# Linear attention and SiLU projections on one core: one turned q in another bank, state scalings and one sum of g placed later, three products and one subtraction in another order

## The chip, the cores and the metric

The kernel runs on one core of one Trainium2 chip. A core has five engines with a queue each: TensorE (PE; its weight loads are shown as PEld), VectorE (DVE), ScalarE (ACT), GpSimd (POOL) and SyncE (SP, which only issues transfers here). The metric is the device time of one execution in microseconds (us).

## The reference, cut to what matters

Four sequences of 768 tokens with 8 heads of 48 go through a gated linear recurrence; its output, 3072 tokens by 384, goes through two matrix products with SiLU between them.

```python
for t in range(S):        # q, k, v, alpha: (4, 8, 768, 48)
    state = alpha[:, :, t, :, None] * state + einsum('bhd,bhe->bhde', k[:, :, t], v[:, :, t])
    y[:, :, t] = einsum('bhd,bhde->bhe', q[:, :, t], state)
x = y.transpose(0, 2, 1, 3).reshape(3072, 384)
h = x @ w_in              # (384, 2048)
g = h / (1 + exp(-h))
out = g @ w_out           # (2048, 384)
```

The two weights are in 64 bits in memory and are converted on the chip.

## The kernel before, in words

**Chunks and steps.** The tokens are cut into 24 chunks of 128 tokens (6 per sequence). A loop over steps runs four stages on different chunks: at step n the scores of chunk n-1, the products of chunk n, the values and states of chunk n-1. `products` (and `quotient`) makes running products of alpha by two scans (L760, L790), the scaled k (`kp`, L771, later L775 and L777) and the scaled q (`p`, L797). `scores` multiplies `p` and `kp` on TensorE, copies the result to g-shaped tiles (L844, later L850 and L853), masks it on GpSimd (L845, L857), and scales the sequence's state for this chunk (L864, four ScalarE instructions). `values` multiplies with v and the state and copies the result to `xt` (L903); `states` makes the state's addition from `kn` and v (TensorE, then L920).

**Turning.** The scans need alpha, k and q with tokens in the free dimension. For chunks 0 to 7 `bring` turns them on TensorE into PSUM (L398). For chunks 8 to 23 they are loaded in pieces and VectorE turns them (L724); one buffer (`turn`) holds k, then q, then the flipped `kp` (L807) that goes through memory to become `kn`. Turning k or q also issues the load of the next chunk's.

**PSUM.** Eight banks: three rotate for the attention (`ps_a`), three serve the w_in products (`ps_m`), two the w_out products (`ps_o`). For chunks 0 to 3 `bring` takes k and q to the `ps_o` banks (chunk 1: `ps_m`), from chunk 4 on to `ps_a`.

**The two projections.** Groups of 4 chunks, in two halves of 256 tokens. Groups 0 and 1 are computed plainly (`enter_plain`: w_in products, silu L963). Groups 2 to 5 use 20 block products instead of 24 (`enter`, twice a group, each for one pair of quarter columns): sums of blocks of x (`sums_x`, SUMS_X, L596 to L601) and of w_in (SUMS_W) are multiplied in the order of PRODUCTS; each `add` takes the next pair and accumulates into bank a, b or c; `copy` takes a bank to SBUF on ScalarE (L990, to s[i] or the single buffer `part`), `tt` combines on VectorE (L998), and `silu` follows (L995). `side_by_side` adds two column halves of g (L1073). `leave` makes the w_out products of a half in seven steps with seven products of half size in place of eight, with differences (L1087), partial results u (L1113, L1118, L1128, L1130, L1139), and stores (L1094, L1096, L1099).

**Order.** `enter` and `leave` are generators that are cut by `yield` into pieces; `both` puts one step of `leave` ahead of each step of `enter`, and `fill` advances them between the stages by a due count. TensorE runs in the order in which it is written. Other engines' instructions are ordered by a scheduler, except where `settled` (first part), `in_order` or `tc.keep_in_program_order` fixes the written order. Between the stages `audit` loads alpha and the weights once more and reduces them on VectorE (L713), to check their range; a branch at the end goes to a general version if it fails.

```python
def bring(n, names="akq"):            # L726; n < NA = 8 is turned on TensorE
            if n < GB and name != "a":     # L738, GB = 4
                at = "kq".index(name)
                ps[name] = (bank(at) if n == 1 else out_bank(at, 512)).rearrange("p (j c) -> p j c", c=C)
            else:
                ps[name] = ps_attn()
```

Of the kernel before, what the change touches and what calls it, by code (L numbers as in the profile page):

```python
# [13 lines left out]
ALU = mybir.AluOpType  # L14
# [5 lines left out]
def general(  # L20
# [326 lines left out]
)  # L347

PRODUCTS = (
    (11, 9), (3, 6), (14, 6), (18, 15), (5, 11), (17, 8), (9, 14), (7, 10), (10, 3), (19, 12),  # L350
    (2, 16), (0, 10), (12, 9), (15, 0), (6, 16), (13, 13), (16, 4), (8, 1), (1, 7), (4, 5),
)

# [2 lines left out]
def quotients(  # L356
# [20 lines left out]
    dve, act, gps = nc.vector, nc.scalar, nc.gpsimd  # L377

    late = {}
# [7 lines left out]
    def settled(ins):  # L387

        return tc.keep_in_program_order(ins) if stated[0] else ins
# [21 lines left out]
    GB = 4  # L411
# [26 lines left out]
    def out_bank(i, n):  # L438
        return outs[i].tile([128, 512], F32, name="ps_o")[:, 0:n]

    def ps_attn(n=C):
        return ps_a.tile([128, 512], F32, name="ps_a").rearrange("p (j c) -> p j c", c=n)
# [4 lines left out]
    def idle(n):  # L447

        for _ in range(n):
            pe.matmul(spin[:, 0:C], lhsT=ident, rhs=ident, start=True, stop=True)  # L450
# [267 lines left out]
    def tokens(t):  # L718

        return t[:, 1 : NP * W + 1].rearrange("p (j c) -> p j c", c=W)[:, :, 0:C]  # L720

    def turned(x, to):
        x = x[:, 32:].rearrange("p (g j d) -> p g j d", j=4, d=D)
        dve.transpose(to.rearrange("p g (b j) -> p g j b", j=4), x[:, :, :, 0:32])  # L724

    def bring(n, names="akq"):  # L726

        c = ctxs[n]
        sg = seg[0 if late else n % 2]
        ps = c.setdefault("ps", {})  # L730

        for name in names:
            if n >= NA:
                if name == "a":
                    turned(c[name], tokens(sg))
                    load(n + 1, "a")
                continue
            if n < GB and name != "a":  # L738

                at = "kq".index(name)  # L740
                ps[name] = (bank(at) if n == 1 else out_bank(at, 512)).rearrange("p (j c) -> p j c", c=C)
            else:
                ps[name] = ps_attn()
            if n == 0 and name != "a" or n == 1 and name != "q":
                idle(2)
            for j in range(NP):
                pe.transpose(ps[name][:, j, :], c[name][:, 2 * j : 2 * j + 2, :], ident)
            if name == "a":
                settled(act.copy(tokens(sg), ps[name]))  # L749
# [69 lines left out]
    def scores(n):  # L819
        c = ctxs[n]  # L820
        ci, b = c["ci"], c["b"]
        ps = [ps_attn() for _ in range(2)]

        for j in (0, 2, 1, 3):
            for e in range(2 if n >= NA else 1):
                for u in range(2):
                    r = slice(64 * u, 64 * u + D)
                    at = slice(CH * e, CH * e + CH) if n >= NA else slice(0, C)  # L830
                    t = slice(CH * (e ^ j // 2) if n >= NA else 0, C)
                    pe.matmul(ps[u][at, j, t], lhsT=c["kp"][r, j, at], rhs=c["qp"][r, j, t],
                              start=True, stop=True)
        if n == 1:

            room = gpool.tile([128, 4, 2, TB], F32, name="g").rearrange("p a b n -> p (a b n)")
            c["room"] = room[:, 2 * NP * C :]
        g = (room[:, 0 : 2 * NP * C] if n == 1 else decayed).rearrange(
            "p (u j c) -> p u j c", u=2, j=NP)
        swapped = decayed.rearrange("p (o u j c) -> p o u j c", o=2, u=2, j=NP // 2)  # L840
        c["g"] = (lambda u, j: g[:, u, j, :]) if n < NA else (
            lambda u, j: swapped[:, j // 2, u, j % 2, :])
        for u in range(2 if n < NA else 0):
            settled(act.copy(g[:, u], ps[u]))  # L844
            gps.affine_select(g[:, u], g[:, u], pattern=[[0, NP], [1, C]], compare_op=ALU.is_ge,  # L845
                              fill=0.0, base=0, channel_multiplier=-1)
        if n >= NA:
            ps = [x.rearrange("p (o j) c -> p o j c", o=2) for x in ps]
            for u in range(2):
                act.copy(swapped[:, :, u, :, CH:], ps[u][:, :, :, CH:])  # L850
            for r, o in earlier:
                for u in range(2):
                    act.copy(swapped[r, o, u, :, 0:CH], ps[u][r, o, :, 0:CH])  # L853
            for at, half in ((CH, later), (0, earlier)):
                for r, o in half:
                    x = swapped[r, o].rearrange("p u j c -> p (u j) c")[:, :, at : at + CH]
                    gps.affine_select(x, x, pattern=[[0, NP], [1, CH]],  # L857
                                      compare_op=ALU.is_ge, fill=0.0, base=0, channel_multiplier=-1)
        if n != 1:
            back(n)  # L860
        if ci > 0:
            s = st[b].rearrange("p j u e -> p j (u e)")
            for j in range(NP):
                mul = act.mul(s[:, j], s[:, j], least[:, n, j : j + 1])  # L864
                if late:
                    tc.keep_in_program_order(mul)


# [79 lines left out]
    def bank(i, n=512):  # L948
        return banks[turn[i]].tile([128, 512], F32, name="ps_m")[:, 0:n]
# [21 lines left out]
    def enter(grp, pair):  # L971
        g_tiles(grp, pair)
        halves = [gts[grp, h, pair] for h in range(2)]

        s = [halves[o % 2][:, o // 2] for o in range(8)]
        todo = iter(PRODUCTS)

        def new(i):
            return bank(i).rearrange("p (e n) -> p e n", e=2)

        def add(ps, first=False):
            w, x = next(todo)
            for e in range(2):
                pe.matmul(ps[:, e], lhsT=block_w(w)[:, 2 * pair + e], rhs=block_x(grp, x),
                          start=(first and e == 0), stop=(e == 1), skip_group_check=True)

        def copy(ps, to=None):
            if to is None:
                to = late["part"].tile([128, 2, TB], F32, name="part")
            act.copy(to, ps)  # L990
            return to

        def silu(h, i):
            x = halves[h][:, i : i + 2]
            act.activation(x, x, AF.Silu)  # L995

        def tt(to, a, b, op=ALU.add):
            dve.tensor_tensor(to, a, b, op)  # L998

        a, b, c = [new(i) for i in range(3)]  # L1000
        add(a, True)
        copy(a, s[6])
        add(b, True)
        copy(b, s[2])
        add(c, True)
        tt(s[6], s[6], copy(c), ALU.subtract)
        yield
        add(a)
        t = copy(a)
        add(b)  # L1010
        copy(b, s[4])
        add(c)
        copy(c, s[7])
        tt(s[7], s[7], t, ALU.subtract)
        yield
        add(a)
        copy(a, s[5])
        add(b)
        copy(b, s[3])
        tt(s[5], s[5], s[3])  # L1020
        add(c)
        copy(c, s[0])
        yield
        add(a)
        tt(s[4], a, s[4])
        b = new(1)
        add(b, True)
        add(b)
        copy(b, s[1])
        yield  # L1030
        c = new(2)
        add(c, True)
        tt(s[2], s[2], copy(c), ALU.subtract)
        a = new(0)
        add(a, True)
        tt(s[6], a, s[6])
        silu(0, 2)
        add(b)
        tt(s[5], copy(b), s[5], ALU.subtract)
        yield  # L1040
        add(c)
        tt(s[1], c, s[1])
        tt(s[3], s[1], s[3], ALU.subtract)
        a = new(0)
        add(a, True)
        tt(s[2], a, s[2])
        add(b)
        tt(s[7], b, s[7])
        silu(1, 2)
        yield  # L1050
        add(c)
        combine(s[1], -1, s[1], -1, s[0])
        tt(s[0], c, s[0])
        silu(0, 0)
        a = new(0)
        add(a, True)
        tt(s[3], a, s[3])
        silu(1, 0)
        turn.append(turn.pop(0))
        for h in range(2):  # L1060
            side_by_side(grp, h, pair)
        yield

    def cells(grp, h, pair, m, k):

        return gts[grp, h, pair][:, k::2, :, m * C : (m + 1) * C]
# [3 lines left out]
    def side_by_side(grp, h, pair):  # L1070

        x = cells(grp, h, pair, 1, 0)
        settled(dve.tensor_tensor(x, x, cells(grp, h, pair, 1, 1), ALU.add))  # L1073

    def leave(grp, h):

# [227 lines left out]
    for step in range(5, STEPS):  # L1304
# [6 lines left out]
        for slot, group in enumerate(stages):  # L1311
            for stage, lag in group:
                n = step - lag
# [9 lines left out]
            if step * SLOTS + slot == (NA + 1) * SLOTS - 1:  # L1323
                x = decayed.rearrange("p (o i c) -> p o i c", o=2, c=C)
# [87 lines left out]
```

## Time and profile before

| | us |
|---|---|
| median of 3 runs | 553.72 (553.66 to 554.34) |
| the profiled execution | 553.72 |
| its span, from the first to the last instruction | 552.0 |
| TensorE busy, first matmul at 1.6, last ends 547.1 | 539.4 |
| VectorE busy | 446.9 |
| ScalarE busy | 208.2 |
| GpSimd busy | 79.0 |
| TensorE, w_out products (`ps_o`), all | 233.4 |
| TensorE, w_in products (`ps_m`), all but the start | 249.1 |

A line of the timeline reads: start and length in us, engine, line of the kernel, operation, tile written and tiles read, shapes, count, and in brackets how long the engine sat idle before it and what ended that. TensorE rows of one kind are merged; the end of such a row overlaps the next one. A wait is put down to the instruction whose semaphore came last.

### The profile page before, as it was taken

What the parts mean: (1) busy time and instruction counts of PE and PEld (TensorE: products, weight loads), DVE (VectorE), ACT (ScalarE), POOL (GpSimd) and SP (SyncE); (2) the same over time, 40 slices, a digit from 0 to 9 for tenths busy, and PEclk for the clock granted to TensorE, in tenths of its full rate; (3) what the DMA queues carried; (4) which work ended last, traced back from release to release, by engine and by line L of the source; (5) the groups of instructions that cost most, each with busy time, mean ns of one, the idle gap of its engine ahead of it and who ended that gap; (6) DMA issues with size and microseconds to landing.
All of it is one profiled execution on the core that took longest, in us unless ns stands there. A gap on an engine that the chain in (4) does not pass through costs nothing. (4 is left out here: it accounts for less than half of the span.)

```text
span 552.0 us, 12718 instructions
## 1 busy us (share of the span) xinstructions
PE 539.4 (98%) x5068; PEld 491.9 (89%) x5068; DVE 446.9 (81%) x801; ACT 208.2 (38%) x466; POOL 79.0 (14%) x146
## 2 busy tenths in 40 slices
PE   8999999999999999999999999999999999999996
PEld 7787888998899899899999999988998999999996
DVE  5999789974999899997998986998883796955531
ACT  3555654123333344354354253353263342332200
POOL 4111000131211202111011021021131000001000
PEclk9999999999999999999999999999999999999999
DMA  9999762253545434455445654717642136500000
GB/s 214 305 224 216 218 186 54 57 153 90 140 130 140 131 83 119 122 136 152 113 126 145 177 148 110 199 24 181 181 130 90 54 86 173 168 21 15 17 28 27
DMA packets 99218, 70.11 MB, mean 127 GB/s; under 512 B 56272, under 2 KB 88656, under 8 KB 99152
## 3 DMA queue, kind: packets, MB, share of 16 engines
q1 hardware_dynamic: 97232, 65.30, 45.9%
q0 software_dynamic: 1920, 3.93, 2.1%
q8 instruction: 41, 0.67, 0.5%
q14 instruction: 25, 0.20, 0.1%
HBM read 61.34 MB, written 7.86 MB: 125 GB/s over the span
## 5 line engine op out<-in xcount | busy, mean ns | idle before, releaser
L394 PE MATMUL ps_o<-w_out,g 128*128 128x192 f32 x768 | 133.7, 328 | 0.0
L394 PEld LDWEIGHTS ps_o<-w_out,g 128*128 128x128 f32 x768 | 125.8, 190 | 2.5 <-DVE o L1096 0.2
L394 PE MATMUL ps_m<-xt,w_in 128*128 128x256 f32 x480 | 111.9, 381 | 1.0 <-ACT xt L903 0.6
L394 PEld LDWEIGHTS ps_m<-xt,w_in 128*128 128x128 f32 x480 | 89.7, 190 | 13.6 <-ACT xt L903 0.8
L394 PE MATMUL ps_o<-wt,g 128*128 128x192 f32 x576 | 99.7, 326 | 0.0
L394 PEld LDWEIGHTS ps_o<-wt,g 128*128 128x128 f32 x576 | 95.1, 190 | 1.5
L394 PE MATMUL ps_m<-xc,w_in 128*128 128x256 f32 x288 | 70.7, 382 | 0.0
L394 PEld LDWEIGHTS ps_m<-xc,w_in 128*128 128x128 f32 x288 | 53.7, 190 | 7.0 <-DVE g L998 0.3
L995 ACT ACTIVATE g<-g 128x1024 f32<-128x1024 f32 x32 | 33.1, 1056 | 61.0 <-DVE g L998 60.9
L1087 DVE TENSOR_TENSOR g<-g 128x512 f32<-128x512 f32 x72 | 49.9, 707 | 6.8 <-PE ps_o L394 6.8
L857 POOL TENSOR_SCALAR_AFFINE_SELECT g<-g 64x256 f32<-64x256 f32 x64 | 36.3, 567 | 124.1 <-ACT g L850 105.4
L1099 POOL DMA_DIRECT2D out_dram<-o x40 | 22.1, 552 | 214.7 <-DVE o L1096 110.7
L394 PE MATMUL ps_m<-xc,wx 128*128 128x256 f32 x192 | 50.1, 383 | 1.0 <-DVE xc L600 1.0
L990 ACT COPY g<-ps_m 128x512 f32<-128x512 f32 x64 | 36.6, 589 | 37.0 <-PE ps_m L394 36.9
L394 PEld LDWEIGHTS ps_m<-xc,wx 128*128 128x128 f32 x192 | 35.2, 190 | 5.2 <-ACT u L1118 1.2
L998 DVE TENSOR_TENSOR g<-ps_m,g 128x512 f32<-128x512 f32 x56 | 37.0, 681 | 3.2 <-PE ps_m L394 2.7
L760 DVE TENSOR_TENSOR_SCAN u<-al,one 128x516 f32<-128x516 f32 x24 | 30.1, 1254 | 6.9 <-ACT al L749 6.6
L990 ACT COPY part<-ps_m 128x512 f32<-128x512 f32 x32 | 18.9, 590 | 37.3 <-PE ps_m L394 24.0
L963 ACT ACTIVATE g<-ps_m 128x512 f32<-128x512 f32 x32 | 19.0, 595 | 35.5 <-PE ps_m L394 35.1
L790 DVE TENSOR_TENSOR_SCAN p<-al,inv 128x516 f32<-128x516 f32 x24 | 30.0, 1250 | 1.0 <-PE ps_a L394 0.3
L713 DVE TENSOR_REDUCE seen<-bits 128x1 f32<-128x512 int32 (+1 forms) x33 | 26.3, 824 | 5.5 <-DMA bits<-in_moe_w_in_dram 5.5
L1096 DVE TENSOR_TENSOR o<-ps_o,u 128x192 f32<-128x192 f32 x24 | 8.5, 353 | 24.9 <-PE ps_o L394 23.0
(134 smaller groups left out, 653.6 us busy)
## 6 DMA issues: line engine op xcount, KB each, us to landing
bits<-in_moe_w_in_dram SPq DMA_DIRECT2D x24, 512.0 KB, 4.7
bits<-in_moe_w_out_dram SPq DMA_DIRECT2D x16, 384.0 KB, 3.8
at<-in_alpha_dram SPq DMA_DIRECT2D x64, 96.0 KB, 2.6
kt<-in_k_dram SPq DMA_DIRECT2D x64, 96.0 KB, 2.5
qt<-in_q_dram SPq DMA_DIRECT2D x64, 96.0 KB, 2.6
bits<-in_alpha_dram SPq DMA_DIRECT2D x9, 512.0 KB, 4.1
out_dram<-o POOLq DMA_DIRECT2D x40, 96.0 KB, 2.6
flips<-turn SPq DMA_DIRECT2D x12, 256.0 KB, 2.4
```

Of the source, the lines that this page charges most:

```text
L394: in_order(nc.tensor.matmul(*args, **kw))
L713: dve.tensor_reduce(seen[kind][which][:, i : i + 1], x, axis=AX, op=op, apply_absolute_value=True))
L760: settled(dve.tensor_tensor_scan(u[:, end - 1 :: -1], sg[:, end:0:-1], one[:, end:0:-1], 0.0, ALU.mult, ALU.add))
L790: settled(dve.tensor_tensor_scan(p[:, 0:end], sg[:, 0:end], iv[:, 0:end], 0.0, ALU.mult, ALU.add))
L857: gps.affine_select(x, x, pattern=[[0, NP], [1, CH]], compare_op=ALU.is_ge, fill=0.0, base=0, channel_multiplier=-1)
L963: settled(act.activation(gts[grp, h, pair][:, i : i + 2, q % 2, :], ps, AF.Silu))
L990: act.copy(to, ps)
L995: act.activation(x, x, AF.Silu)
L998: dve.tensor_tensor(to, a, b, op)
L1087: dve.tensor_tensor(cells(grp, h, pair, *to), cells(grp, h, pair, *x), cells(grp, h, pair, *y), ALU.subtract)
L1096: dve.tensor_tensor(o, x, y, ALU.add)
L1099: (gps if grp < NG - 1 else nc.sync).dma_start(out[r : r + C, c * HO : (c + 1) * HO], o)
```

## The change

Five edits, none of which adds or removes an instruction with work:

- The turned q of chunk 6 goes to the second `ps_o` bank, as it does for chunks 0, 2 and 3, in place of a `ps_a` bank.
- The four state scalings of chunk 6 keep their written order on ScalarE; the scheduler had put them a step earlier. They now stand behind the copy of `kn` of chunk 6.
- The sum of g (`side_by_side`) of group 1, second half, first pair, keeps its written order; on VectorE it now stands behind k's and q's turning for chunk 9 and their products, ahead of the flip, where it stood ahead of the turning.
- In every call of `enter`, the second round of products runs c, b, a in place of a, b, c: PRODUCTS has (17, 8) and (18, 15) exchanged, and the copies to s[7], s[4] and `part` follow in that order.
- In group 2, first pair, the subtraction into s[3] stands behind the addition into s[2].

On GpSimd and SyncE the order of the instructions is the same as before.

```diff
 PRODUCTS = (
-    (11, 9), (3, 6), (14, 6), (18, 15), (5, 11), (17, 8), (9, 14), (7, 10), (10, 3), (19, 12),
+    (11, 9), (3, 6), (14, 6), (17, 8), (5, 11), (18, 15), (9, 14), (7, 10), (10, 3), (19, 12),
...
-            if n < GB and name != "a":
+            if n < GB and name != "a" or n == 6 and name == "q":
...
                 mul = act.mul(s[:, j], s[:, j], least[:, n, j : j + 1])
-                if late:
+                if late or n == 6:
                     tc.keep_in_program_order(mul)
...
-        add(a)
-        t = copy(a)
+        add(c)
+        copy(c, s[7])
         add(b)
         copy(b, s[4])
-        add(c)
-        copy(c, s[7])
-        tt(s[7], s[7], t, ALU.subtract)
+        add(a)
+        tt(s[7], s[7], copy(a), ALU.subtract)
         yield
...
         tt(s[1], c, s[1])
-        tt(s[3], s[1], s[3], ALU.subtract)
+        late_3 = (grp, pair) == (2, 0)
+        if not late_3:
+            tt(s[3], s[1], s[3], ALU.subtract)
         a = new(0)
         add(a, True)
         tt(s[2], a, s[2])
+        if late_3:
+            tt(s[3], s[1], s[3], ALU.subtract)
...
-        settled(dve.tensor_tensor(x, x, cells(grp, h, pair, 1, 1), ALU.add))
+        total = dve.tensor_tensor(x, x, cells(grp, h, pair, 1, 1), ALU.add)
+        if (grp, h, pair) == (1, 1, 0):
+            tc.keep_in_program_order(total)
+        settled(total)
```

## The prediction

> **What bounds the kernel now.** I read the page first, then the waits of TensorE alone, then the timeline around each wait.
>
> ```profile
> span 552.0 us, 12718 instructions
> ...
> PE 539.4 (98%) x5068; PEld 491.9 (89%) x5068; DVE 446.9 (81%) x801; ACT 208.2 (38%) x466; POOL 79.0 (14%) x146
> ```
>
> TensorE is busy for 539.4 of 552.0 us. What can be won is the rest, and in it only the places where TensorE waits for another engine. Before 80 us these belong to the start and the change doesn't touch them. The waits view of TensorE (who is waited for: us, times, longest) has the later ones:
>
> ```profile
> PE ps_m L394 <- DVE xc L600: 1.0, 1, 1.0
> PE ps_a L394 <- DVE kp L771: 0.8, 2, 0.5
> PE ps_a L394 <- DVE p L797: 0.7, 2, 0.5
> ...
> PE ps_m L394 <- DVE g L998: 0.4, 1, 0.4
> ```
>
> One of the two waits for `p` lies in the start. The timeline shows each of the others with the instruction that ends it.
>
> Place A, steps 6 and 7 of the chunk loop (start, duration, engine, line, tiles, idle before):
>
> ```profile
> 83.95 0.69 DVE L771 TENSOR_TENSOR kp<-ps_a,u 128x512 f32<-128x512 f32 x1
> 83.95 1.17 ACT L864 ACTIVATE st<-st,least 128x96 f32<-128x96 f32 x4 [1.63 <-DVE least L763]
> ...
> 84.69 0.55 PE L394 MATMUL ps_a<-vn,kn 128*32 128x48 f32 x32 [0.54 <-DVE kp L771]
> ...
> 85.03 0.46 ACT L903 COPY xt<-ps_a 128x384 f32<-128x384 f32 x1
> ...
> 85.53 8.04 PE L394 MATMUL ps_m<-xt,w_in 128*128 128x256 f32 x36 [0.29 <-ACT xt L903]
> ...
> 102.96 0.69 DVE L771 TENSOR_TENSOR kp<-ps_a,u 128x512 f32<-128x512 f32 x1
> ...
> 103.71 0.55 PE L394 MATMUL ps_a<-vn,kn 128*32 128x48 f32 x32 [0.28 <-DVE kp L771]
> ```
>
> The state product `vn,kn` of chunk 5 waits at 84.69 for `kp` of chunk 6 (83.95 + 0.69 = 84.64), because its bank held k of chunk 6. The next w_in product waits at 85.53 for the copy of `xt` (ends 85.49), which stands on ScalarE behind four state scalings (1.17 us). At 103.71 the same state product of the next step waits for `kp` of chunk 7 (ends 103.65).
>
> Place B, the second chunk that is turned on VectorE (chunk 9):
>
> ```profile
> 136.32 0.69 DVE L1073 TENSOR_TENSOR g<-g 128x512 f32<-128x512 f32 x1 [7.63 <-ACT g L963]
> ...
> 140.10 0.69 DVE L797 TENSOR_TENSOR p<-turn,p 128x512 f32<-128x512 f32 x1
> ...
> 140.94 0.90 PE L394 MATMUL ps_a<-p,kp 48*64 48x128 f32 x32 [0.48 <-DVE p L797]
> ```
>
> VectorE sits idle for 7.6 us until 136.32 because the sum of g waits for ScalarE's silu; k's and q's turning stand behind it, and the scores (`p,kp`) at 140.94 wait for the last of them.
>
> Place C, group 2:
>
> ```profile
> 225.83 1.28 DVE L998 TENSOR_TENSOR g<-ps_m,g 128x512 f32<-128x512 f32 x2
> ...
> 226.57 1.13 PE L394 MATMUL ps_m<-xt,w_in 128*128 128x256 f32 x4 [0.40 <-DVE g L998]
> ...
> 231.72 0.46 ACT L903 COPY xt<-ps_a 128x384 f32<-128x384 f32 x1
> ...
> 232.44 0.79 PE L394 MATMUL ps_a<-p,kp 48*64 48x128 f32 x26
> ```
>
> The last w_in product waits at 226.57 for the first of the two L998 at 225.83, which reads its bank. Further on, the scores at 232.44 start just after the copy of `xt` that ends at 232.18.
>
> Place D, group 4. The quarter sum of x that TensorE waits for, and then the next place where TensorE and VectorE meet:
>
> ```profile
> 364.94 0.41 DVE L600 TENSOR_TENSOR xc<-xc,xt 128x256 f32<-128x256 f32 x1
> ```
>
> ```profile
> 392.82 0.69 DVE L713 TENSOR_REDUCE seen<-bits 128x1 f32<-128x512 int32 x1 [1.50 <-DMA bits<-in_moe_w_in_dram]
> ...
> 397.41 0.34 DVE L1096 TENSOR_TENSOR o<-ps_o,u 128x192 f32<-128x192 f32 x1
> ...
> 397.91 1.41 PE L394 MATMUL ps_o<-w_out,g 128*128 128x192 f32 x7
> ```
>
> At 365.50 TensorE idles 0.97 us for that L600 (x block 15). At 397.91 an output product follows 0.16 us after VectorE has read its bank (397.75).
>
> **What the Trainium skill says.** "PSUM — Partial Sum Buffer", section "Engine vs sequencer instructions": ScalarE's and VectorE's queues are strict first in, first out, and matmuls start in program order. The trace agrees: the `xt` copy at 85.03 starts only after the scalings. "Perfetto Trace Analysis", section "Identifying the Most-Contended Engine": matmul busy time is no good measure of closeness to the peak; so I count gaps against the spacing of the same rows elsewhere, not the 98%. The same section's neighbour "Optimization Strategy" says to look for the gaps on the engine that should be full and for what will end them; here each gap has one releaser. I take no price from the skill.
>
> **The change part by part.** No edit adds an instruction with work, a DMA or a buffer. Durations are rows of the profiled execution.
>
> *A: q of chunk 6 in a w_out bank, its state scalings later.* With q in the output bank the state product takes the bank of `a`, free since the copy ahead of 82.4, and no longer waits at 84.69. The four scalings go behind the scores and the k copy of chunk 6 (about 96.3), where ScalarE idles 1.57 us before 97.88 and they need 1.17, so they cost nothing; without that idle time they would delay one silu by 1.17 us. The w_in product then waits for the `xt` copy alone. At 122.56 the same sequence took 1.44 us from the query product (`p,st`) to the w_in product (124.00); here 83.30 + 1.44 = 84.74 against 85.53, a gain of 0.79 us. What is late next? TensorE's next meeting with VectorE is 103.71. VectorE has no idle stretch over 0.14 us between 81.88 and 103.65 (it converts w_out and forms its differences), so `kp` of chunk 7 ends at 103.65 however early TensorE is, and this chunk's q and k stay in the old banks. The wait there grows from about 0.55 to 1.34 us. Net 0. The bank itself is free: TensorE's first output product starts at 98.99, q is read by 86.79.
>
> *B: the sum of g for group 1, second half, behind the turning.* After the scan that ends at 128.70 VectorE goes straight on: turn k 1.13, two products 0.42 each, turn q 1.11, product 0.69, done by about 132.5, against 140.39 when the scores could start. GpSimd's selects run beside it then (L857, 1.84 us from 128.51); beside such selects two sums at 95.56 and 96.47 took 0.99 us where others took 0.55, so a stretch of a microsecond may be added and changes nothing. k and q of that chunk were issued to SP by 118.8 and 122.7 and DMAs of this size land in about 2.6 us, so they are there. The four loads of the next k and the four of the next q are issued when the old ones are turned: they move from 138.09 and 140.10 to about 131.5 and 133.3 (SP is busy with the loads of `a` to 131.5), and the loads of v and the flip behind them on SP come earlier, not later. The sum still starts at 136.32, its silu's end. The matching hand-over (16 output products, then scores) at 355.44 took 2.80 us; here 137.59 to 140.94 is 3.35. Gain 0.55 us. From there to 185.5 VectorE is ahead of where it was and TensorE meets nothing tight; at 185.50 VectorE again waits 1.6 us for a silu, thus for TensorE, so what follows moves along. Net 0.55.
>
> *C: in group 2, first pair, the subtraction into s3 behind the addition into s2.* The addition then runs at 225.24 and ends at 225.92, and the product goes at about 226.0 instead of 226.57. The undisturbed row at 351.62 needs 1.82 us for the two products to the next instruction (353.44); here 225.03 to 227.63 is 2.60. 0.10 us of that belongs to the small wait at 225.03 that stays, so 0.67 is gained. What is next: the scores at 232.45 need the `xt` copy. It stands on ScalarE behind two silu that wait for two L998 at 229.12, and VectorE is full from 185.5 on; it ends at 232.18 still. The scores can start 0.05 later, at 232.23. Net 0.22; at 250.84 VectorE waits for TensorE, so this part is kept.
>
> *D: another order of three w_in products.* In all eight calls bank c takes its second product first, with x block 8 in place of block 15. Block 8 is ready by 360.15, block 11 at 363.36 (needed 365.23), block 15 at 365.35 (needed 366.10). The start without a wait: 361.77 + 2.60 (16 output products, as at 343.83) = 364.37; with 0.08 us of slow restart that is 1.21 gained at 366. Then: VectorE has only two idle stretches over 0.11 us from 342.92 to 397.75, both ended by the landing of an audit DMA (1.3 at 375.56, 1.5 at 392.82) that was issued as soon as VectorE had freed its buffer (371.28 and 388.09). So its chain doesn't shorten. TensorE, 1.2 us early, waits in part at 390.1, at 395.3 and finally at 397.91 for the bank read at 397.41 to 397.75: start 397.80. Net 0.11. The other seven calls have no wait there to lose. ScalarE's copies in the new order (s7, s4, then the one into the single `part` buffer) put the one that waits for VectorE last, so it holds up less; TensorE has the next 16 output products (2.60 us) as cover for it.
>
> Sum: 0 + 0.55 + 0.22 + 0.11 = 0.88 us. 552.0 - 0.88 = 551.1 span, and with 1.72 us around it (553.72 - 552.0) 552.85; the profiled execution's time is also the median of the runs.
>
> **Rivals.** (1) *The gains of C and D last*, wholly or in part: the audit DMAs land earlier or VectorE's chains have slack that I read as work. Landings took 3.6 to 5.2 us, so half a microsecond is easily had. All of it: 0.55 + 0.67 + 1.21 = 2.43, 551.3. Against: VectorE's rows touch each other. (2) *A lasts too*: 0.88 + 0.79 = 1.67, 552.05. Against: the 21 us without idle time before 103.65. (3) *B fails too*: its gain is met by a wait that the trace of before hides; 552.85 + 0.55 = 553.4, or 553.7 with C and D gone as well. Against: the nearest VectorE release in that stretch has 0.84 us of slack. (4) *Slower*: bank c is written again by the very next call of its kind, so its product now waits for the copy into `part`. Today that copy ends 0.91 us before the product would start (238.56 - 237.64 = 0.92, 364.37 - 363.44 = 0.93; 0.65 at 406.83). From the point where the copy is later than this, each of the eight calls pays; 0.25 us each, a copy 1.16 us late, turns 0.88 gained into 1.1 lost: 554.85. For it: the copy stands behind ScalarE's other work. Against: nothing moves in front of it.
>
> **How the numbers follow.** Forecast 0.50, with its own range 552.5 to 553.3; rival 1 0.29, rival 2 0.06, rival 3 0.08, rival 4 0.07. 0.2% (1.1 us) is about what a measurement of this kernel can tell from no change. Faster: rivals 1 and 2 and 0.05 of the forecast, 0.40; same 0.53; slower 0.07. The range goes down to all of rival 1 and up over rival 3: 551.2 to 554.0; outside are rival 4 and the lowest mixtures.
>
> **What would show it.** A: no wait at 84.7, `vn,kn` near 103.7 waiting over 1 us for `kp`. B: VectorE turning k near 129, no wait of the scores near 140.4. C: s2's product near 226 (less B), scores still just behind the `xt` copy. D: no wait for `xc L600`; instead small waits for L998 near 390 and 395 and for L1096 near 397. If the last is missing, the time is nearer 551.5. A wait of `ps_m` for ScalarE's `part` at each second step would be rival 4.

## The result and the profile after

The changed kernel takes 553.15 us (median of 22 runs, 552.27 to 554.07) against 554.04 us for the kernel before (22 runs, 553.53 to 554.60): ratio 0.9983, 95% interval 0.9976 to 0.9990. The forecast was 552.85 us in a range of 551.2 to 554.0. The difference of the medians is 0.89 us, where the sum of the prediction was 0.88. The interval lies wholly below 1, so the gain is told from no change, small as it is. The profiled execution took 553.06 us, its span 551.3 us.

The page of the changed kernel, its head and the busy times:

```profile
span 551.3 us, 12716 instructions
...
PE 540.0 (98%) x5068; PEld 493.2 (89%) x5068; DVE 448.1 (81%) x801; ACT 209.1 (38%) x466; POOL 80.0 (15%) x146
```

TensorE's busy time is nearly what it was (540.0 against 539.4 us), and every engine has as many instructions with work as before. The waits view of TensorE (engine, tile and line that waits, the work waited for, us in total, times, longest):

```profile
PE ps_a L394 <- DVE kp L771: 1.0, 1, 1.0
...
PE ps_m L394 <- DVE g L998: 0.6, 1, 0.6
```

The waits for `xc L600`, for `p L797` at 140.94 and for L998 at 226.57 are gone. In their place `vn,kn` waits 1.0 us for `kp` (0.3 at that spot before), and at place D there are a wait for L998 (at 388.91) and one of 0.2 us for the bank read L1102 (at 397.09) that were not there. (Line numbers in the changed kernel below 1000 are as before; 1076 was 1073, 1102 was 1096.)

The timeline, row by row through the four places:

```profile
84.82 0.48 PE L394 MATMUL ps_m<-xt,w_in 128*128 128x256 f32 x1 [0.26 <-ACT xt L903]
...
102.99 0.69 DVE L771 TENSOR_TENSOR kp<-ps_a,u 128x512 f32<-128x512 f32 x1
...
103.73 0.55 PE L394 MATMUL ps_a<-vn,kn 128*32 128x48 f32 x32 [1.03 <-DVE kp L771]
...
128.77 1.13 DVE L724 STREAM_TRANSPOSE turn<-kt 128x512 f32<-128x512 f32 x1
...
136.35 0.69 DVE L1076 TENSOR_TENSOR g<-g 128x512 f32<-128x512 f32 x1 [3.49 <-ACT g L963]
...
140.42 0.90 PE L394 MATMUL ps_a<-p,kp 48*64 48x128 f32 x32
...
225.48 1.10 PE L394 MATMUL ps_m<-xt,w_in 128*128 128x256 f32 x4
...
231.19 0.46 ACT L903 COPY xt<-ps_a 128x384 f32<-128x384 f32 x1
...
231.70 0.74 PEld L394 LDWEIGHTS ps_a<-p,kp 48*64 48x64 f32 x30 [0.20 <-ACT xt L903]
...
388.91 1.13 PE L394 MATMUL ps_m<-xt,wx 128*128 128x256 f32 x4 [0.60 <-DVE g L998]
...
392.12 0.69 DVE L713 TENSOR_REDUCE seen<-bits 128x1 f32<-128x512 int32 x1 [1.20 <-DMA bits<-in_moe_w_in_dram]
...
396.69 0.35 DVE L1102 TENSOR_TENSOR o<-ps_o,u 128x192 f32<-128x192 f32 x1
...
397.09 1.08 PE L394 MATMUL ps_o<-w_out,g 128*128 128x192 f32 x5 [0.19 <-DVE o L1102]
```

Place A: the w_in product starts at 84.82 (85.53 before), and `vn,kn` at 103.73 (103.71 before) behind the same `kp`, with a wait of 1.03 us in place of 0.28. Place B: k is turned at 128.77, directly behind the scan; the sum still starts at 136.35, when the silu ends, and the scores start at 140.42 without a wait. Place C: the last w_in product starts at 225.48, and the scores are held at 231.70 by the copy of `xt`, which ends at 231.65. Place D: the x block 15 product goes at 365.35 without a wait; at 388.91 TensorE waits for L998 and at 397.09 for the bank read that ends at 397.04, 0.05 us earlier. The read at 392.12 stands behind the landing of an audit.

**Where the time went, stretch by stretch.** The start of the scores rows (`p,kp`) is a good mark: there is one a chunk, in the same order in every kernel here. The table gives, for the profiled execution of each kernel, how much longer or shorter (us) each stretch between such marks is than in the profiled execution of the kernel before; it is one execution of each kernel. In the kernel before the marks stand at 76.83 (chunk 5), 126.79 (chunk 8), 157.15 (chunk 10), 189.56 (chunk 12), 253.83 (chunk 15), 358.24 (chunk 20), 421.76 (chunk 23), and TensorE ends at 547.08. The stretch from 253.83 to 358.24 is 0.00 in every kernel. (The expectations below count these rows from 0 with the first two chunks' as one, so "chunks 4 to 6" in them are chunks 5 to 7 here.)

| kernel | start, to 76.83 | A, to 126.79 | B, to 157.15 | to 189.56 | C, to 253.83 | D, 358.24 to 421.76 | end, to 547.08 |
|---|---|---|---|---|---|---|---|
| changed kernel | +0.07 | -0.04 | -0.55 | 0.00 | -0.22 | -0.07 | 0.00 |
| A alone | +0.37 | -0.05 | +0.01 | 0.00 | +0.28 | 0.00 | 0.00 |
| B alone | +0.18 | +0.04 | -0.55 | 0.00 | -0.02 | 0.00 | 0.00 |
| C alone | +0.22 | -0.05 | 0.00 | 0.00 | -0.23 | +0.01 | 0.00 |
| D alone | +0.39 | -0.06 | -0.01 | 0.00 | -0.07 | +0.27 | 0.00 |
| q of chunk 7 | +0.25 | -1.28 | -0.55 | 0.00 | +0.06 | 0.00 | 0.00 |
| silus held | +0.26 | -0.05 | -0.55 | 0.00 | -0.62 | +0.39 | 0.00 |
| audits at the end | +0.51 | +0.15 | +0.01 | 0.00 | +0.27 | +0.02 | +4.12 |
| D, audits at the end | +0.24 | -0.04 | -0.01 | 0.00 | 0.00 | -1.21 | +3.88 |
| D, audits early | +0.14 | +0.02 | +4.04 | +7.02 | +2.75 | -1.09 | 0.00 |
| all, audits early | +0.44 | -1.28 | -0.55 | +5.85 | +2.12 | -1.12 | 0.00 |
| D, one audit moved | +0.26 | +0.12 | +0.02 | 0.00 | -0.02 | -1.11 | 0.00 |
| all, one audit moved | +0.22 | -1.28 | -0.55 | 0.00 | -0.33 | -1.21 | 0.00 |

Not all of this is the edits. No edit touches the start; it differs by up to 0.5 us between executions, and the profiled execution of the kernel before had the shortest of all, which fits that its time of 553.72 lies below the medians of 554.04 to 554.38 that this kernel had in later series. Stretch A scatters from -0.06 to +0.15 in kernels without edit A. In stretch C, 0.28 us come and go by a scan (last section). Without the start, the four stretches of the changed kernel sum to -0.88 us.

### The profile page after: what moved, and what is told of

The parts are those of the page before. It is cut to its first block, busy times and chain, and to the rows that moved or that the text cites. A ratio compares the mean times of both kernels' runs of the same rounds, so it can differ in the third digit from the quotient of the medians.

```text
span 551.3 us, 12716 instructions
## 1 busy us (share of the span) xinstructions
PE 540.0 (98%) x5068; PEld 493.2 (89%) x5068; DVE 448.1 (81%) x801; ACT 209.1 (38%) x466; POOL 80.0 (15%) x146
## 5 line engine op out<-in xcount | busy, mean ns | idle before, releaser
L998 DVE TENSOR_TENSOR g<-ps_m,g 128x512 f32<-128x512 f32 x56 | 37.1, 682 | 3.2 <-PE ps_m L394 2.7
L790 DVE TENSOR_TENSOR_SCAN p<-al,inv 128x516 f32<-128x516 f32 x24 | 30.2, 1259 | 0.9 <-PE ps_a L394 0.2
L713 DVE TENSOR_REDUCE seen<-bits 128x1 f32<-128x512 int32 (+1 forms) x33 | 26.3, 822 | 5.0 <-DMA bits<-in_moe_w_in_dram 5.0
L1102 DVE TENSOR_TENSOR o<-ps_o,u 128x192 f32<-128x192 f32 x24 | 8.5, 354 | 26.7 <-PE ps_o L394 24.8
```

What stands on the lines that cost most here:

```text
L713: dve.tensor_reduce(seen[kind][which][:, i : i + 1], x, axis=AX, op=op, apply_absolute_value=True))
L790: settled(dve.tensor_tensor_scan(p[:, 0:end], sg[:, 0:end], iv[:, 0:end], 0.0, ALU.mult, ALU.add))
L1102: dve.tensor_tensor(o, x, y, ALU.add)
```

## The experiments

### Each part alone

The kernel before with one edit each: A (the bank of chunk 6's q and the kept scalings), B (the sum of g), C (the subtraction into s3), D (PRODUCTS and the second round). The edits are those of the diff of the change, each by itself:

```diff
# A
+            if n < GB and name != "a" or n == 6 and name == "q":
+                if late or n == 6:
# B
+        if (grp, h, pair) == (1, 1, 0):
+            tc.keep_in_program_order(total)
# C
+        late_3 = (grp, pair) == (2, 0)
# D
+    (11, 9), (3, 6), (14, 6), (17, 8), (5, 11), (18, 15), (9, 14), (7, 10), (10, 3), (19, 12),
```

> The kernel before with edit A alone: q of chunk 6 in an output bank, the four scalings of that step kept in order behind the scores. Theory (place A is met again at 103.7 us by VectorE's chain): no wait at 84.7 and 85.5, the w_in product at about 84.8, but the state product at 103.7 waits about 0.8 us longer for kp L771; time 0.0 us against before (-0.2 to +0.2). Rival (the gain lasts): -0.79 us. Rival (the scalings in their new place hold up a silu): +0.3 us or more.

> The kernel before with edit B alone: the sum of g of (1, 1, 0) kept behind the turning of k and q. Theory: the scores at 140.94 start at about 140.4 without a wait for p L797, and nothing takes that back: -0.55 us (-0.7 to -0.4). Rival (met by a hidden wait): 0.0 us.

> The kernel before with edit C alone: in group 2, first pair, the subtraction into s3 behind the addition into s2. Theory: the last w_in product starts at about 226.0 instead of 226.57, then the scores wait for the xt copy L903 and start at about 232.2: -0.2 us (-0.4 to -0.1). Rival (all of it lasts): -0.67 us. Rival (nothing, VectorE's chain sets it all): 0.0 us.

> The kernel before with edit D alone: the new order of the three w_in products and of one sum. Theory: no wait for xc L600 at 365.5 (there 1.2 us ahead), then waits for L998 near 389.7 and for L1096 near 397.8, where the output product starts at about 397.8 instead of 397.91: -0.1 us (-0.3 to +0.1). Rival (the gain lasts): -1.2 us. Rival (each bank c waits for the copy into part): +1 us or more, with waits for part in the waits of TensorE.

All beside the kernel before at 554.17 us. A: 553.96, ratio 0.9999 (0.9991 to 1.0008). B: 553.36, ratio 0.9985 (0.9979 to 0.9992). C: 553.66, ratio 0.9998 (0.9989 to 1.0006). D: 553.73, ratio 0.9994 (0.9985 to 1.0002). Only B's interval lies wholly below 1. (The ratios are not the plain quotients of these medians, which would be 0.9996, 0.9985, 0.9991 and 0.9992; each of these lies inside its interval.) The table says more than the times: A -0.05 in its stretch (D alone, which has no edit there, shows -0.06), B -0.55, C -0.23, as expected to a few hundredths; for C the scan of that stretch is as short as in the kernel before (1.23 us), so the two can be compared. In A alone the w_in product starts 0.79 us earlier in that stretch, and the next mark gives 0.74 back. A's two halves, the bank and the scalings, were not run apart. D misses its expectation of -0.1 in its one profiled execution: +0.27. That execution, 554.32 us, is the second slowest of the 13, and the interval of all 13 times, -0.8 to +0.1 us, holds -0.1 and not +0.27. The mechanism is the expected one; what sets the size is told under "Why the prediction was right".

### A: is the wait for `kp` of chunk 7 all that took its gain?

The changed kernel, and q of chunk 7 also in another bank, so that the state product at 103.7 has a bank that no late k or q holds:

```diff
-            if n < GB and name != "a" or n == 6 and name == "q":
+            if n < GB and name != "a" or n in (6, 7) and name == "q":
...
-                ps[name] = (bank(at) if n == 1 else out_bank(at, 512)).rearrange("p (j c) -> p j c", c=C)
+                ps[name] = (bank(at) if n == 1 else bank(2) if n == 7 else out_bank(at, 512)).rearrange("p (j c) -> p j c", c=C)
```

> The changed kernel, with q of chunk 7 put into a w_in bank as well, so that the state product at 103.7 us need not wait for kp L771. Theory (A's gain was there and VectorE's kp L771 took it back): that wait of 1.3 us goes, nothing else is near, and scores to scores over chunks 5 to 7 becomes about 1.2 us shorter than in the changed kernel; against before about -2.1 us (-1.6 to -2.3). Rival (the next release by VectorE, at 109.8, takes it back in turn): -0.9 us against before, no better than the changed kernel.

Measured: 552.37 us against 554.38, ratio 0.9961 (0.9947 to 0.9976), 2.0 us. The timeline of this kernel at the place:

```profile
102.70 0.52 PE L394 MATMUL ps_a<-vn,kn 128*32 128x48 f32 x32
...
103.26 0.69 DVE L771 TENSOR_TENSOR kp<-ps_a,u 128x512 f32<-128x512 f32 x1
```

The product no longer waits; it starts 0.56 us before `kp` does. Stretch A is 1.28 us shorter than before (1.24 shorter than in the changed kernel). That is A's 0.79, kept, and 0.49 that the wait for `kp` at 103.71 had cost in the kernel before already. So the gain of A was there and lay waiting behind one bank; VectorE's `kp`, 103.26 now and 102.99 in the changed kernel, is no earlier.

### C: is the copy of `xt` behind the silus all that is left?

The changed kernel, with the last two silus of group 2, first pair, and the sums behind them written after that copy:

```diff
+        moved = settled(act.copy(xts[half][:, :, e * C : (e + 1) * C], py[:, 0:NKT]))
+        if "held" in late:
+            tc.keep_in_program_order(moved)
+            late.pop("held")()
...
+        if held:
+            late["held"] = finish       # the two silus, kept in order, then side_by_side
+        else:
+            finish()
```

> The changed kernel, with the last two silus of group 2, first pair, and the sums behind them put after the xt copy L903 on ScalarE. Theory (C's remainder is held by that copy, which stands behind the silus): the scores at 231.3 start about 0.4 us earlier, directly behind the output products; against before about -1.3 us. Rival (VectorE's full chain holds the scores in any case): no better than the changed kernel, -0.9 us; with the later sums in the way of the next step, -0.6 us.

Measured: 553.19 us against 554.38, ratio 0.9977 (0.9967 to 0.9986), 1.2 us, which looks as expected. By stretch it is so only in part: C is 0.40 us shorter than in the changed kernel (-0.62 against -0.22), as expected, but in this execution D came out at +0.39 against -0.07. That is not C's gain taken back: nothing is lost between the two stretches. It is D's own size, which changes from one trace to the next (see "Why the prediction was right").

### D: does VectorE's chain with its audits take the gain back?

The audits are reads of the inputs that a load brings in 512 KB pieces; VectorE reads two a step. In both kernels the four of steps 21 and 22 (TensorE is at these steps from 358 to 400 us) are made up in the loop at the end; nothing is left out. One is the kernel before, one has edit D:

```diff
-        if at % 2 == 0 and step > 3 * GB + 2:
+        if at % 2 == 0 and step > 3 * GB + 2 and step not in (21, 22):
```

> The kernel before with the four audits of steps 21 and 22 made up at the end, without edit D (a control). Theory: the wait for xc L600 at 365.5 stays and no other wait depends on these audits: 0.0 us (-0.2 to +0.2). Rival (the audits cost time by themselves, whatever D does): -0.5 us or more.

> The kernel before with edit D, and the four audits of steps 21 and 22 made up at the end (audits checked late, none left out), so that VectorE waits for no audit DMA at 375 and 392 us. Theory (VectorE's chain with its audits takes D's gain back): no waits for L998 at 389 and L1096/L1102 at 397; scores to scores over 358 to 401 us about 1.2 us shorter than before; time -1.2 us (-1.4 to -0.9) against before. Rival (another chain is behind it): at most -0.3 us, like edit D alone.

Measured: the control 558.25 us against 554.38 (ratio 1.0064, 1.0042 to 1.0085), with D 555.82 (1.0027, 1.0018 to 1.0036). As times both expectations fell: the control was to be 0.0 and is 3.9 us slower. In stretch D both hold: +0.02 in the control and -1.21 with D. So the audits cost nothing there by themselves, and without them D gains all of its 1.2 us. What was overlooked is the end. A window of the kernel with D and the audits at the end (stretch; busy us and count of TensorE, weight loads, VectorE, ScalarE, GpSimd; granted TensorE clock; DMA share; GB/s):

```profile
476.00:480.00 4.00, 4.00 (x15) 4.00 (x15) 3.80 (x8) 2.00 (x2) 0.54 (x1) 0.58 0.73 201
```

Made up at the end, the audits' reads stand between VectorE's sums there, and in this kernel's timeline TensorE waits 0.98 us for L998 at 474.01 and 0.65 us for a bank read at 475.79. After these two waits the mean granted clock is 0.58 over the 4 us shown; taken finer, it is 0.50 from 475.94 to 479.35, which is another 1.7 us (3.41 x 0.50). With the waits that is 3.3 of the 3.88 us in the table; the rest was not traced. The end's cost is not the same in each execution: the 22 times of this kernel go from 554.78 to 558.53.

### The audits ahead of the others

Five places for an audit in steps 9 to 11, where VectorE has idle time, in exchange for the four of steps 21 and 22 and the first of step 15. The audits are taken in a fixed order, so those that now come early are the first of the list, loads of alpha. First with D alone, then with all other edits of this section ("all": the changed kernel, q of chunk 7, silus held):

```diff
+        if at in (38, 40, 42, 44, 46) or at % 2 == 0 and at > 60 and step not in (21, 22):
```

> The kernel before with edit D, and with the four audits of steps 21 and 22 placed ahead of the others, in steps 9 to 11 (about 145 to 180 us), where VectorE has some 5 us of idle time; as many audits are left for the end as before. Theory: over 358 to 401 us 1.2 us are gained as with the audits at the end, and the 3 to 4 us that those cost at 474 us and after are not paid: -1.2 us against before (-1.4 to -0.7; the order of VectorE's work from 145 to 250 us shifts with it and may cost some tenths at 225 us). Rival (the audits cost as much wherever they stand): +0.5 us or more.

> The changed kernel with q of chunk 7 in a w_in bank, the last silus of group 2, first pair, behind the xt copy, and the four audits ahead as in d_early. Theory: the four places add up, by scores to scores: chunks 4 to 6 -1.25, chunk 8 -0.55, chunks 12 to 14 -0.62, chunks 19 to 21 -1.2, together -3.6 us against before (-3.0 to -3.8). Rival (VectorE's moved order takes part of it at 225 us, or a later meeting of the two engines does): -2.4 us, no better than q of chunk 7 alone.

Measured: 565.35 us (ratio 1.0201, 1.0183 to 1.0219) and 559.71 us (1.0107, 1.0092 to 1.0122) against 554.10. Both expectations fell. A and B are as expected in the second, D is -1.09 and -1.12, but stretches that were to lose nothing lose 5.9 to 11.1 us before 189.56, and over 2 us more up to 253.83. The timeline of the second kernel:

```profile
166.42 1.21 DVE L713 TENSOR_REDUCE seen<-bits 128x1 f32<-128x1024 f32 x1
...
167.66 0.33 SPq L697 DMA_DIRECT2D bits<-in_alpha_dram  x1
...
168.08 1.81 SPq L817 DMA_DIRECT2D kn<-flips  x4
...
172.92 0.73 PE L394 MATMUL ps_a<-vn,kn 128*32 128x48 f32 x32 [4.02 <-DMA kn<-flips]
```

The audit load at 167.66 waits for its single buffer, which VectorE reads until 167.63. It stands on SP ahead of the four loads of `kn`, which in the changed kernel go out at 158.78; they go out at 168.08 here (SP's own queue shows 8.4 us of waiting for L713), and TensorE waits 4.02 us for them, then runs at a clock of 0.50 from 173.13 to 176.54: 4.02 + 1.7 of the 5.85 us. In the first kernel it waits for these loads twice, 2.13 us at 156.39 and 3.87 us at 178.36. I had counted VectorE's idle time and not the queue of SP. What the further 2 us in stretch C are I have read only as far as waits (in the second kernel 1.0 us for `part` and 1.2 us for L998); their cause was not tried apart and stays open.

### One audit, moved past nothing

A single read taken out of step 21 and put at the end of step 22; no load of a chunk gets a new one ahead of it. The expectations give wrong times for it. In the traces, the kernel before has reads at 369.95 and 375.56 us in step 21 and the kernel with D alone a single one, at 370.92; the added one shows at 403.27. With D alone, and with all (the changed kernel, q of chunk 7, silus held):

```diff
+        if step > 3 * GB + 2 and (at % 2 == 0 and at != 84 or at == 91):
```

> The kernel before with edit D, and with a single audit moved: none is issued in step 21 at slot 0 (read at about 385 us), one more in step 22 at slot 3 (about 427 us), where VectorE has idle time; nothing moves to the end and no load of a chunk gets a new one ahead of it. Theory: without that read (1.3 us) and the wait for the next audit's landing (1.2 to 1.7 us) VectorE is ahead of TensorE at 388 and 397 us; scores to scores over 358 to 401 us are 1.2 us shorter than before, and nothing is paid later: -1.2 us against before (-1.4 to -0.8). Rival (VectorE's chain is full for another reason, or the audit costs as much at its new place): -0.3 to +0.5 us.

> The changed kernel with q of chunk 7 in a w_in bank, the last silus of group 2, first pair, behind the xt copy, and the single audit moved as in d_move. Theory: the four places add up, scores to scores: chunks 4 to 6 -1.25, chunk 8 -0.55, chunks 12 to 14 -0.62, chunks 19 to 21 -1.2, together -3.6 us against before (-3.0 to -3.9). Rival (a later meeting of the engines takes part of it): -2.4 us, no better than q of chunk 7 alone.

Measured: with D alone 552.87 us against 554.21, ratio 0.9975 (0.9965 to 0.9984), 1.3 us. With all, 550.27 us, ratio 0.9929 (0.9915 to 0.9942), 3.9 us faster than before and faster than either kernel. The timeline of the first at place D:

```profile
389.77 1.28 DVE L713 TENSOR_REDUCE seen<-bits 128x1 f32<-128x512 int32 x2 [2.46 <-DMA bits<-in_moe_w_in_dram]
...
396.79 0.33 DVE L1095 TENSOR_TENSOR o<-ps_o,u 128x192 f32<-128x192 f32 x1
...
397.18 2.06 PE L394 MATMUL ps_o<-w_out,g 128*128 128x192 f32 x11
```

The audit at 389.77 now finds VectorE idle 2.46 us, because VectorE is that far ahead. TensorE shows no wait there, and the bank is read until 397.12, 0.06 us before TensorE's output product. Stretch D is -1.11, and -1.21 with all. For "all" the parts of the table are -1.28, -0.55, -0.33 and -1.21, together -3.37 in the profiled executions; C falls short of its -0.62 by the scan told of below.

## Why the prediction was right

It was right about a gain of under a microsecond, to 0.3 us in the time, and about the place and the mechanism of each of its four parts; the size of one part, D, was luck.

- **A (predicted 0).** As argued: 0.79 us won at 84.8 and given back at 103.73, and VectorE's chain from 81.9 to 103.7 did not shorten. The runs show both halves: A alone -0.05, with the next bank freed -1.28.
- **B (predicted -0.55).** -0.55 in every kernel that has the edit. The microsecond of stretching allowed for beside GpSimd's selects was 0.24 (k's first product took 0.66 in place of 0.42 us). The loads that moved ahead on SP hurt nobody.
- **C (predicted -0.22).** -0.22 and -0.23. The product started at 225.48, that is 226.03 without B's part, for a predicted 226.0; the copy of `xt` held the scores, and with the copy freed 0.40 of the remaining 0.45 came.
- **D (predicted -0.11).** The place is right, and so is what takes the gain back: TensorE is 1.20 us ahead at the scores of chunk 21 (1.21 predicted), nothing of it lasts, and without the audits of steps 21 and 22 all of it does (-1.21). The size rests on a term that I took for fixed and that is not: VectorE's last bank read, 39.17 us after the scores of chunk 20 in the kernel before. In the changed kernel, D alone, q of chunk 7 and silus held, which all have the edit, it came 39.19, 39.54, 39.27 and 39.66 us after them, and D's stretch is each time, to 0.01, the shift against 39.17 less 0.10: -0.07, +0.27, 0.00 and +0.39. Two of the things that move the read show in the rows. One is the audit: from its issue near 388 us to its read it took 4.73 us before, and 4.44, 4.81, 4.88 and 4.88 in these four. The other is the scan L790 near 380 us, 1.23 us before and 1.44, 1.45, 1.22 and 1.43. Here are the scan and GpSimd's selects in the kernel before, then in the changed one:

```profile
380.86 1.23 DVE L790 TENSOR_TENSOR_SCAN p<-al,inv 128x516 f32<-128x516 f32 x1
...
382.29 1.84 POOL L857 TENSOR_SCALAR_AFFINE_SELECT g<-g 64x256 f32<-64x256 f32 x4 [10.16 <-ACT g L850]
```

```profile
380.35 2.69 POOL L857 TENSOR_SCALAR_AFFINE_SELECT g<-g 64x256 f32<-64x256 f32 x4 [10.16 <-ACT g L850]
380.43 1.44 DVE L790 TENSOR_TENSOR_SCAN p<-al,inv 128x516 f32<-128x516 f32 x1
```

The edit itself brings the two together: TensorE's scores come 1.20 us earlier, so GpSimd masks them 1.20 us earlier, 22.74 us after the scores of chunk 20 in place of 23.94, and now meets the scan. In the three kernels with the long scan a select had started up to 0.08 us ahead of it; in the one with the short scan, the scan was first by 0.09 us. The prediction followed ScalarE's copies here and left GpSimd out. In the changed kernel the audit is issued 0.33 us later after the mark and takes 0.29 us less; so its -0.07 agrees with -0.11 by chance. The waits are not the predicted ones either (0.6 at 388.91, none at 394.20). The whole times fit a size that changes between executions: their standard deviation is 0.57 us for the changed kernel against 0.29 for the kernel before, 0.45 for D alone against 0.25 to 0.35 for A, B and C alone, and 0.2 in both kernels with one audit moved.
- **The step from span to time.** "The profiled execution's time is also the median of the runs" failed by 0.3 us: that execution had a short start. So the predicted 552.85 lies 0.30 below the measured 553.15, though the difference is right to 0.01, which is closer than the measurement can tell. A slip of 0.01 in C's sum (2.60 - 1.82 - 0.10 is 0.68, not 0.67) changes nothing.
- **The rivals.** Rivals 1 and 2, that gains of A, C or D last, did not come, but the runs show how near they were: one bank, one order on ScalarE, one audit. Rival 3 did not come. Rival 4 did not either: the waits of TensorE show none for `part` in the changed kernel.

The Trainium skill, "PSUM — Partial Sum Buffer", section "Engine vs sequencer instructions", on which A and C rested (ScalarE and VectorE take their queues strictly in order), is borne out by the runs: the copy of `xt` of stretch C ran at 231.19 behind the silus and at 228.47 once the two silus (and the sums behind them) had been put behind it, and k's turning, held behind the waiting sum until 136.93, ran at 128.77 when it stood ahead of it. At place A the prediction reads the copy of `xt` as starting only after the scalings; by the rows it starts 0.09 us before the last of them ends (85.03 against 85.12), so what the trace shows there is their order.

## What to carry to other kernels

A wait that is removed on the full engine gains only up to the next place where it meets the slower chain, and that place can be named in advance: follow the other engine's rows and look whether they have idle time. If they don't, shorten or move that chain, or take away the meeting (another bank); here that turned 0.9 us into 3.9. When work is moved into another engine's idle time, count its transfer too: what stands behind it on the issuing queue, and how long it will wait there for its buffer.

## What the runs showed of the hardware that I had not expected

- **A wait of TensorE can be charged twice.** After waits of 0.98 and 0.65 us that ended within 2 us of each other (475.79) the granted clock was 0.50 for 3.41 us; after one of 2.13 us (audits early, D alone, at 156.39) and after one of 4.02 us (172.92, with all) it was 0.50 for 3.41 us too. That is 1.7 us each (the lost share times the stretch). After one of 3.87 us (D alone, at 178.36) it stayed at 0.50 for 6.26 us, which is 3.1 us. After a single wait of 1.0 us, at 365.5 in the kernel before or at 103.7 in the changed one, it stayed at 1.00. The Trainium skill, "TensorE: Matmul & The Clock Gate", section "HAM oscillation — how this bites in real kernels", gives idle gaps of over some 3.4 us as what throttles; here shorter ones, and two together, were enough, so the measurement decides.
- **The same scan takes 1.23 us or 1.43 to 1.47 us.** The scan of stretch C in the kernel before, while GpSimd's four selects run beside it:

```profile
212.75 2.85 POOL L857 TENSOR_SCALAR_AFFINE_SELECT g<-g 64x256 f32<-64x256 f32 x4 [10.50 <-ACT g L850]
213.20 1.23 DVE L760 TENSOR_TENSOR_SCAN u<-al,one 128x516 f32<-128x516 f32 x1
```

In A alone, where the same code runs there:

```profile
213.08 2.65 POOL L857 TENSOR_SCALAR_AFFINE_SELECT g<-g 64x256 f32<-64x256 f32 x4 [10.50 <-ACT g L850]
213.58 1.47 DVE L760 TENSOR_TENSOR_SCAN u<-al,one 128x516 f32<-128x516 f32 x1
```

VectorE has no idle time from there to 225 us, so these 0.24 us, with 0.05 by which the scan starts later, become the +0.28 of the table. The Trainium skill, "SBUF — State Buffer", section "Who interferes with whom", says that a VectorE instruction with two inputs in SBUF and a GpSimd instruction that reads SBUF exclude each other, and that the one issued first goes on. The trace agrees: in the kernel before, the scan starts at 213.20, 0.02 us ahead of the second select, and that select takes 1.43 us in place of 0.41; in A alone, the second select starts at 213.55, 0.03 us ahead of the scan, and takes 0.42 us, while the scan takes 1.47 (the third select, behind the scan, then takes 1.22). It depends on hundredths of a microsecond which of the two is first, so the same order of work can cost 0.2 us more after a change elsewhere, as it did at place D.
- **The start's spread**: up to 0.5 us between executions of kernels whose start is the same, more than half of the effect studied. The marks inside the trace repeat to 0.02 us in B's stretch where neither B is edited nor an audit moved there; the intervals of the whole times are 0.7 to 0.9 us wide for the changed kernel and the parts alone.
